# One-hots of a token inversion: GpSimd builds one of the two for six batches of eight, DVE builds the other with wide comparisons

## The chip, the cores and the metric

The kernel runs on one core of one Trainium2 chip. The metric is the device time of one execution in microseconds. Five engines work side by side, each through its own instructions in its own order: TensorE (PE; its weight loads are shown apart as PEld), VectorE (DVE), ScalarE (ACT), GpSimd (POOL) and SyncE (SP, which here only starts DMAs). An instruction waits for what it needs from the others, and everything behind it on its engine waits with it.

## The reference

Eight batches of 3584 tokens with 192 channels go through a causal depthwise convolution, with 7 taps and one softmaxed filter for each of 8 heads. All 28672 convolved tokens then go to a mixture of experts: a token whose skip score is positive goes to the one of 8 experts with the largest logit and has that expert's result, times the gate, added.

```python
def _attn_ref(x, weight):                      # x (8, 3584, 192), weight (8, 7)
...
    out = np.einsum('hk,bskhg->bshg', w, x_unf)
    return out.reshape(B, S, D).astype(np.float32)

def _moe_ref(x, w_skip, w_gate, w1, w2):       # w1 (8, 192, 1024), w2 (8, 1024, 192)
    skip_score = x @ w_skip
    do_compute = skip_score > 0
    out = x.copy()
    xc = x[do_compute]
    logits = xc @ w_gate
    e_idx = np.argmax(logits, axis=1)
...
    for e in range(E):
        mask = e_idx == e
        h = np.maximum(xc[mask] @ w1[e], 0.0)
        y[mask] = gate_w[mask, None] * (h @ w2[e])
    out[do_compute] = xc + y
```

## The kernel before, in words

**Phase 1** has eight steps, one for each batch. A batch lies in SBUF as 30 columns (`NC`) of 120 tokens (`R`), token within the column on the partition. In its step each of the 8 heads is convolved on PE (`pc`, L333, two matmuls a head with a band matrix) and copied by ACT into `ys` (L335); SP loads the input of the batch two steps on (`load_x`, which has two small memsets on POOL, L113 and L114, before its loads L115 to L121) and stores `ys` to the output (`store_y`, L383 and L386). Between the heads of one step stands the work on the batch before: `router` (transposes `tp`, L419; the odd channel parts are first copied to `yc`, by POOL at L398 for batches 0 to 5; logits `pl`, `pb`) and `route` (on DVE: the largest logit, the gate, and by a running count the slot that each token gets in its expert's list). A slot is a row `r` of 128 and a column `q`: `ri`, `qi`, then `rf`, `qf` as floats (L557, L559).

**The inversion** (`invert`) turns "slot of a token" into "token of a slot". For each of the 30 columns of a batch it builds two tables by comparison: `oa` (120 tokens x 128 rows; 1 where the row is the token's row) and `ob` (120 x 144; 1 where the column is the token's). One of the two carries the token's number as value, taken from `vtab` (the program's `vtab32`). The matmul `inv += oa^T ob` (L581) puts each number at its slot in PSUM; 30 matmuls for a batch, accumulating over batches 0 to 4 and then over 5 to 7. Before, DVE builds both: one `tensor_scalar` for each column and table, in groups of four columns (`IC`).

**The order is written by hand.** `invert` and the other pieces are generators; a `yield HOP` ends a turn. The tables `RR`, `IR` and `BGS` say how many turns of routing, of inversion and of background work follow each head, and `PICK` in which order two routings and an inversion take turns. Background work is the preparation of expert weights: load, maximum on DVE (`am`, `ar`), an all-reduce over partitions on POOL (`sc`, L262), powers of two on DVE (L305 to L310), scaled halves on ACT and DVE. In phase 1 it is done for two experts (the all-reduces beside batch 0's inversion and late in step 5). The products of a group of columns come one turn (`lag`) after its tables, in the tail two.

**The tail.** After the inversion of batch 4 (`REL`), lists for two experts (`sidxa`) are cut out, and POOL begins with indirect DMAs: gathers of 128 tokens each (`y`, L739) and of their gates (`g`, L747), after the memsets of their tiles (L726, L727), and later scatters of the results (`out_dram`, L816). Eight blocks of these experts (up-projection `ph` L792 with ACT `hh` and DVE `hl`, down-projection `po` L827 to L842) run on PE while batches 6 and 7 are routed and batches 5 to 7 inverted. Then come the final lists (`sidx`) and **the steady part**, one block behind the other on PE.

## Time and profile before

| | |
|---|---|
| median of 3 runs | 726.39 us (724.96 to 727.82) |
| the profiled execution | 726.94 us, span 724.9 us |
| PE busy, whole span | 675.7 us (93%) |
| DVE busy | 596.3 us (82%) |
| POOL busy | 391.4 us (54%) |
| DVE, tables `oa` and `ob` (240 instructions each) | 59.2 us and 48.7 us |
| PE, matmuls `inv` (240) | 29.9 us |
| start of the memset at the end of step 2 (input of batch 4), and of the first at the end of step 6 (tiles of the tail) | 75.53 us, 184.67 us |

A row of the timeline has the start, the duration, engine, line, operation, output tile<-input tiles, shape and count; in brackets stands the engine's idle time before it and who ended that. A row of the groups has the count, then busy time of all, the mean of one (which overlaps its neighbours, since an engine starts an instruction before the last has ended), and the idle time before them. In a row of the stretches stand the busy times of PE, PEld, DVE, ACT and POOL with their instructions, the clock granted to PE (1.00 is full), the DMA share, and GB/s.

### The profile page before, as it was taken

To read this page: it belongs to the slowest core of one execution; us is meant where nothing else is said; L and a number is where in the kernel's file an instruction comes from. 1 tells how busy PE (TensorE), PEld (TensorE's weight loads), DVE (VectorE), ACT (ScalarE), POOL (GpSimd) and SP (SyncE) were. 2 spreads that over 40 slices of the span, in tenths; PEclk is the share of its full clock that TensorE was granted. 3 is DMA by queue.
4 is the path that set the end of the run, shared out by engine and by line. 5 is a ranking of instruction groups with operands and counts; after the bars stand their busy time and mean duration, and the time that the engine had idled before them with its cause. 6 is when DMAs were issued, how large, how long until landed. Compare 5 with 4: busy or idle time off the path is not lost.

```text
span 724.9 us, 16759 instructions
## 1 busy us (share of the span) xinstructions
PE 675.7 (93%) x5768; PEld 537.6 (74%) x5768; DVE 596.3 (82%) x1917; ACT 319.8 (44%) x654; POOL 391.4 (54%) x434
## 2 busy tenths in 40 slices
PE   5989699798989888999999999999999999999994
PEld 4656466575668778988888888888888888888883
...
GB/s 227 170 268 291 233 241 292 250 211 241 90 213 194 53 110 109 155 112 146 168 123 183 123 165 162 92 174 179 86 180 147 126 127 152 291 279 300 294 181 12
...
## 3 DMA queue, kind: packets, MB, share of 16 engines
...
## 4 chain that ended last, share of the span: by engine, by line
PE 61%; DVE 7%; DMA 1%; ACT 0%; issue 0%; POOL 0%; POOLq 0%; DVEq 0%
PE ph L792 32%; PE po L827 18%; PE po L830 9%; DVE oa L590 2%; PE po L842 2%; DVE ob L596 1%; DVE hl L797 1%; DMA m<-yt 1%; DMA y<-out_dram,sidx 1%; DVE o L813 0%; DVE yt L766 0%; DVE yam L756 0%; PE tp L419 0%; ACT hh L795 0%; PE inv L581 0%
## 5 line engine op out<-in xcount | busy, mean ns | idle before, releaser
L795 ACT ACTIVATE hh<-ph 128x512 f16<-128x512 f32 x230 | 132.9, 590 | 223.7 <-PE ph L792 215.3
L792 PE MATMUL ph<-m,wt 128*128 128x256 f16 (+1 forms) x2000 | 221.0, 269 | 6.0 <-DVE hl L797 4.7
L792 PEld LDWEIGHTS <-wt 128*128 128x128 f16 x2000 | 189.0, 98 | 30.2 <-issue 7.4
L827 PE MATMUL po<-wt,hh 128*128 128x384 f16 x656 | 167.5, 326 | 0.0
L797 DVE SCALAR_TENSOR_TENSOR hl<-ph,hh 128x512 f16<-128x512 f32 x230 | 155.5, 686 | 10.5 <-ACT hh L795 8.9
L830 PE MATMUL po<-wt,hl 128*128 128x192 f16 x656 | 147.5, 246 | 0.0
L827 PEld LDWEIGHTS <-hh 128*128 128x128 f16 x808 | 78.3, 98 | 39.7
L747 POOL DMA_INDIRECT g<-gate_dr,sidx x82 | 87.3, 1065 | 25.0 <-issue 24.1
L739 POOL DMA_INDIRECT y<-out_dram,sidx x82 | 84.1, 1026 | 27.0 <-issue 18.6
L816 POOL DMA_INDIRECT out_dram<-o,sidx x82 | 84.6, 1031 | 25.1 <-issue 5.8
L830 PEld LDWEIGHTS <-hl 128*128 128x128 f16 x808 | 79.1, 98 | 10.2
L333 PE MATMUL pc<-xs,toep 128*120 128x360 f32 x224 | 84.0, 499 | 0.0
L813 DVE SCALAR_TENSOR_TENSOR o<-po,yf,y 128x192 f32<-128x192 f32 x115 | 47.3, 415 | 42.2 <-PE po L827 35.0
L761 ACT ACTIVATE yt<-y,ysc 128x192 f16<-128x192 f32 x115 | 46.4, 447 | 70.5 <-DVE ysc L310 51.8
L335 ACT COPY ys<-pc 120x720 f32<-120x720 f32 x56 | 42.5, 759 | 58.8 <-PE pc L333 37.4
L766 DVE SCALAR_TENSOR_TENSOR yt<-y,ysc,yt 128x64 f16<-128x64 f32 x230 | 58.2, 313 | 1.9 <-ACT yt L761 1.7
L590 DVE TENSOR_SCALAR oa<-iota_r,rf,vtab 120x128 f16<-120x128 f16 x240 | 59.2, 315 | 0.0
L333 PEld LDWEIGHTS pc<-xs,toep 128*120 128x120 f32 x224 | 39.1, 195 | 16.8 <-issue 3.6
L596 DVE TENSOR_SCALAR ob<-iota_q,qf 120x144 f16<-120x144 f16 x240 | 48.7, 264 | 0.0
L813 DVE SCALAR_TENSOR_TENSOR o<-po,yf,o 128x192 f32<-128x192 f32 x101 | 42.2, 418 | 3.6
L286 DVE SCALAR_TENSOR_TENSOR wt<-raw,ar,wt 128x512 f16<-128x512 f32 x56 | 41.6, 744 | 4.1 <-ACT wt L275 4.1
L256 DVE TENSOR_REDUCE am<-raw 128x1 f32<-128x512 f32 x56 | 37.8, 677 | 7.7 <-DMA raw<-in_moe_w_dram 7.4
...
## 6 DMA issues: line engine op xcount, KB each, us to landing
...
```

Source lines behind the costliest of these rows:

```text
L333: nc.tensor.matmul(pc[0:R, i, 0:n * G], toep[:, h, :], xs[:, c0 + n * i:c0 + n * i + n, h * G:(h + 1) * G], start=True, stop=True)
L590: nc.vector.tensor_scalar(out=oa[:, v, :], in0=iota_r[0:R], scalar1=rf[:, c0 + v:c0 + v + 1], scalar2=vtab32[0:R, c0 + v:c0 + v + 1], op0= ...
L739: rows_apart(nc.gpsimd.indirect_dma_start(out=k.y[:, u, :], out_offset=None, in_=out[0:k.rows, :], in_offset=bass.IndirectOffsetOnAxis(ap= ...
L747: nc.gpsimd.indirect_dma_start(out=k.g[:, u:u + 1], out_offset=None, in_=gate_dr[0:k.rows, :], in_offset=bass.IndirectOffsetOnAxis(ap=k.si ...
L766: nc.vector.scalar_tensor_tensor(out=yt[:, u, o:o + b_ - a], in0=k.y[:, u, a:b_], scalar=sc[:, u:u + 1], in1=yt[:, u, a:b_], op0=ALU.mult, ...
L792: nc.tensor.matmul(ph[:, f - f0, :], wt[:, o + f * P:o + (f + 1) * P], k.m[:, m, 0:w], start=(n == 0), stop=(n == len(seq) - 1))
L795: nc.scalar.activation(hh, ph, AF.Relu)
L797: nc.vector.scalar_tensor_tensor(out=k.hl[:, f0:f0 + fs, 0:w], in0=ph, scalar=0.0, in1=hh, op0=ALU.max, op1=ALU.subtract)
L813: nc.vector.scalar_tensor_tensor(out=o[:, u, :], in0=part, scalar=f2[:, u:u + 1], in1=base, op0=ALU.mult, op1=ALU.add)
L816: rows_apart(nc.gpsimd.indirect_dma_start(out=out[0:k.rows, :], out_offset=bass.IndirectOffsetOnAxis(ap=k.si[:, u:u + 1], axis=0), in_=o[: ...
L827: nc.tensor.matmul(po, k.hh[:, f, u * P:(u + 1) * P], w2[:, f], start=(f == 0), stop=(f == NF - 1))
L830: nc.tensor.matmul(po[:, 1], k.hl[:, f, u * P:(u + 1) * P], w2[:, f, 0], start=False, stop=False)
```

## The change

`IC` goes from 4 to 8 columns, worked in two half-turns of four columns, and the tables have three buffers of eight columns instead of four of four. For batches 0 to 5 POOL builds `ob`, one `tensor_scalar` a column, now with the value, so 30 a batch and 180 in all (new L600); DVE builds `oa` with one wide `tensor_tensor` for eight columns (120 x 1024, L609) and no value. For batches 6 and 7 DVE builds both wide: `oa`, `oa` times the value, `ob`. `rf` becomes f16, and so does `qf` in batches 6 and 7; an f16 table of the values is added. The products of a group of eight come after both of its half-turns, four in each turn.

```diff
--- before.py
+++ after.py
@@ -28,7 +28,7 @@
 LAST = S - R * (NC - 1)
 NG = NC // 2
 HALVES = ((0, 16), (16, NC - 16))
-IC = 4
+IC = 8
 SPAN = 32768
 QC = 18
 NQ = E * QC
@@ -63,6 +63,7 @@
 PICK = "102"
 E1 = 3
 PSEQ = (0, 0, 3, 4, 4, 4, 4, 4)
+ONE_HOTS_BY_GPSIMD = (0, 1, 2, 3, 4, 5)
 TLAG = 2
 HOP = -1
 
@@ -204,6 +205,9 @@
                             fill=0.0, base=0, channel_multiplier=1)
     iota_r = const.tile([P, P], F16, name="iota_r")
     iota_q = const.tile([P, NQ], F16, name="iota_q")
+    vtab = const.tile([P, NC], F16, name="vtab")
+    nc.gpsimd.iota(vtab, pattern=[[R, NC]], base=-(S // 2), channel_multiplier=1,
+                   allow_small_or_imprecise_dtypes=True)
     vtab32 = const.tile([P, NC], F32, name="vtab32")
     nc.gpsimd.iota(vtab32, pattern=[[R, NC]], base=-(S // 2), channel_multiplier=1,
                    allow_small_or_imprecise_dtypes=True)
@@ -553,9 +557,9 @@
         nc.vector.tensor_scalar(out=qi, in0=si, scalar1=7, scalar2=None, op0=ALU.arith_shift_right)
         nc.vector.tensor_tensor(out=eq3(cmp), in0=stab, in1=bstart[:, b].unsqueeze(2).broadcast_to([P, E, QC]),
                                 op=ALU.is_ge)
-        rf = t2("rf", F32, 2)
+        rf = t2("rf", F16, 2)
         nc.vector.tensor_copy(rf, ri)
-        qf = t2("qf", F32, 2)
+        qf = t2("qf", F32 if b in ONE_HOTS_BY_GPSIMD else F16, 2)
         nc.vector.tensor_copy(qf, qi)
         rq[b] = (rf, qf, gt)
         if b < B - 1:
@@ -570,37 +574,58 @@
 
     def invert(b, rf, qf, gt):
 
+        def each(table, n):
+            return table[0:R].unsqueeze(1).broadcast_to([R, ic, n])
+
+        def along(t, n):
+            return t[0:R, c0:c0 + ic].unsqueeze(2).broadcast_to([R, ic, n])
+
         lag = TLAG if in_tail else 1
+        by_gpsimd = b in ONE_HOTS_BY_GPSIMD
         due = []
 
         def products(at):
             if due and due[0][0] <= at:
-                _, c0, oa, ob = due.pop(0)
-                for v in range(min(IC, NC - c0)):
+                _, c0, v0, oa, ob = due.pop(0)
+                for v in range(v0, min(v0 + IC // 2, NC - c0)):
                     w = c0 + v
                     nc.tensor.matmul(inv, oa[:, v, :], ob[:, v, :],
                                      start=(b in (0, REL + 1) and w == 0), stop=(b in (REL, B - 1) and w == NC - 1))
 
+        def columns(v0):
+
+            if by_gpsimd:
+                for v in range(v0, min(v0 + IC // 2, ic)):
+                    w = c0 + v
+                    nc.gpsimd.tensor_scalar(out=ob[:, v, :], in0=iota_q[0:R], scalar1=qf[:, w:w + 1],
+                                            scalar2=vtab32[0:R, w:w + 1], op0=ALU.is_equal, op1=ALU.mult)
+
         at = 0
         for c0 in range(0, NC, IC):
             ic = min(IC, NC - c0)
-            oa = wk1.tile([R, IC, P], F16, tag="oa", bufs=4, name=f"oa{b}_{c0}")
-            ob = wk1.tile([R, IC, NQ], F16, tag="ob", bufs=4, name=f"ob{b}_{c0}")
-            for v in range(ic):
-                nc.vector.tensor_scalar(out=oa[:, v, :], in0=iota_r[0:R], scalar1=rf[:, c0 + v:c0 + v + 1],
-                                        scalar2=vtab32[0:R, c0 + v:c0 + v + 1], op0=ALU.is_equal, op1=ALU.mult)
+            oa = wk1.tile([R, IC, P], F16, tag="oa", bufs=3, name=f"oa{b}_{c0}")
+            ob = wk1.tile([R, IC, NQ], F16, tag="ob", bufs=3, name=f"ob{b}_{c0}")
+            columns(0)
+            nc.vector.tensor_tensor(out=oa[:, 0:ic, :], in0=each(iota_r, P), in1=along(rf, P), op=ALU.is_equal)
             if c0 == 0:
                 store_gates(b, gt)
             yield
-            for v in range(ic):
-                nc.vector.tensor_scalar(out=ob[:, v, :], in0=iota_q[0:R], scalar1=qf[:, c0 + v:c0 + v + 1],
-                                        scalar2=None, op0=ALU.is_equal)
+            if not by_gpsimd:
+                nc.vector.tensor_tensor(out=oa[:, 0:ic, :], in0=oa[:, 0:ic, :], in1=along(vtab, P), op=ALU.mult)
             products(at)
-            due.append((at + lag, c0, oa, ob))
+            at += 1
+            yield HOP
+            columns(IC // 2)
+            if not by_gpsimd:
+                nc.vector.tensor_tensor(out=ob[:, 0:ic, :], in0=each(iota_q, NQ), in1=along(qf, NQ), op=ALU.is_equal)
+            products(at)
+            due.extend((at + lag, c0, v0, oa, ob) for v0 in (0, IC // 2))
             at += 1
             yield HOP
         while due:
             products(at)
+            if lag == 1:
+                products(at)
             at += 1
             if due:
                 yield HOP
```

Line numbers with the change are one to four higher up to `invert` (L113 is L114, L262 is L266, L333 is L337, L398 is L402, L419 is L423) and 25 higher behind it (L739 is L764, L816 is L841); L581 is L592.

POOL around the first all-reduce (`sc`), in step 2, before. `ISA` alone is the instruction that loads code for POOL; the one with `sc` is the all-reduce.

```order
50 L398 COPY yc_0_566<-ys_346 120x1024
51 L398 COPY yc_1_595<-ys_346 120x896
52 L262 ISA
53 L262 ISA sc_734<-ar_732 128x2
54 L113 MEMSET xs_810 8x192
55 L114 MEMSET xs_810 32x192
56 L398 COPY yc_0_885<-ys_514 120x1024
```

The same place with the change; the tables `ob` are batch 0's, and the number behind `ob_` is the group's first column.

```order
52 L402 COPY yc_1_597<-ys_348 120x896
53 L600 TENSOR_SCALAR ob_0_638<-iota_q,qf_634,vtab_193 120x144 x8
54 L600 TENSOR_SCALAR ob_8_707<-iota_q,qf_634,vtab_193 120x144 x4
55 L266 ISA
56 L266 ISA sc_720<-ar_718 128x2
57 L600 ISA
58 L600 TENSOR_SCALAR ob_8_707<-iota_q,qf_634,vtab_193 120x144 x4
59 L600 TENSOR_SCALAR ob_16_761<-iota_q,qf_634,vtab_193 120x144 x8
60 L114 MEMSET xs_781 8x192
61 L115 MEMSET xs_781 32x192
62 L600 TENSOR_SCALAR ob_24_824<-iota_q,qf_634,vtab_193 120x144 x4
63 L402 COPY yc_0_853<-ys_516 120x1024
```

The all-reduce and two loads of code now stand in the midst of batch 0's tables, and the memset of the next input behind 24 of its 30 columns. Between the tables of batches 2 and 3 the second all-reduce has such a load on either side too:

```order
82 L600 TENSOR_SCALAR ob_24_1416<-iota_q,qf_1233,vtab_193 120x144 x2
83 L266 ISA
84 L266 ISA sc_1462<-ar_1460 128x2
85 L402 COPY yc_1_1481<-ys_1092 120x896
86 L600 ISA
87 L600 TENSOR_SCALAR ob_0_1527<-iota_q,qf_1523,vtab_193 120x144 x8
```

Before, no load of code stood there, and none before the first all-reduce of the steady part, where one stands now.

POOL at the start of the tail, with the change, from the last gathers of the first row of gathers on; the tables are batch 5's:

```order
119 L764 DMA y_2003<-out_dram,sidxa 128x192
120 L772 DMA g_2000<-gate_dr,sidxa 128x1 x2
121 L764 DMA y_2007<-out_dram,sidxa 128x192 x2
122 L600 TENSOR_SCALAR ob_0_2189<-iota_q,qf_2185,vtab_193 120x144 x8
123 L600 TENSOR_SCALAR ob_8_2281<-iota_q,qf_2185,vtab_193 120x144 x8
124 L600 TENSOR_SCALAR ob_16_2350<-iota_q,qf_2185,vtab_193 120x144 x8
125 L600 TENSOR_SCALAR ob_24_2457<-iota_q,qf_2185,vtab_193 120x144 x6
126 L764 DMA y_2011<-out_dram,sidxa 128x192 x2
127 L841 DMA out_dram<-o_2724,sidxa 17920x192 x2
```

Fifteen gathers stand ahead of batch 5's tables, and the others behind all 30 columns. PE at the place of batch 5's first products in step 7 (`pc_6` is head 6 of batch 7, `pl_1`, `pb` and `tp` batch 6's routing), before:

```order
622 L419 MATMUL tp_1_3_2411<-ident,ys_1806 128x120 x2
...
624 L581 MATMUL inv<-ob_0_2357,oa_0_2356 128x144
...
631 L333 MATMUL pc_5_0_2440<-xs_1798,toep 120x360 x2
632 L450 MATMUL pb_0_2444<-ident,lt_0_2403 120x128 x2
633 L419 MATMUL tp_1_4_2450<-ident,yc_1_2311 128x120 x4
```

And with the change:

```order
622 L423 MATMUL tp_1_3_2240<-ident,ys_1675 128x120 x2
623 L337 MATMUL pc_5_0_2259<-xs_1667,toep 120x360 x2
624 L454 MATMUL pb_0_2263<-ident,lt_0_2232 120x128 x2
625 L423 MATMUL tp_1_4_2269<-ident,yc_1_2143 128x120 x4
626 L423 MATMUL tp_1_5_2275<-ident,yc_1_2143 128x120 x3
...
628 L592 MATMUL inv<-ob_0_2189,oa_0_2188 128x144
...
635 L337 MATMUL pc_6_0_2300<-xs_1667,toep 120x360 x2
```

The first products come one head later than before.

## The prediction

> **What bounds the kernel now.** I read the page's busy shares first, then the stretches of ten microseconds, PE's waits, and last the rows of POOL, because the change moves work onto it.
>
> ```profile
> PE 675.7 (93%) x5768; PEld 537.6 (74%) x5768; DVE 596.3 (82%) x1917; ACT 319.8 (44%) x654; POOL 391.4 (54%) x434
> 80.00:90.00 10.00, 4.80 (x19) 3.80 (x20) 5.88 (x24) 4.78 (x9) 0.00 (x0) 0.67 0.86 249
> 160.00:170.00 10.00, 7.82 (x52) 5.67 (x49) 9.70 (x36) 8.73 (x18) 1.23 (x1) 1.00 1.08 336
> 240.00:250.00 10.00, 7.90 (x68) 6.79 (x68) 9.93 (x42) 1.77 (x4) 3.52 (x4) 0.83 0.15 41
> 260.00:270.00 10.00, 7.59 (x71) 6.23 (x70) 9.83 (x42) 2.36 (x5) 4.09 (x4) 1.00 0.49 116
> 300.00:310.00 10.00, 10.00 (x92) 8.62 (x91) 9.72 (x34) 3.81 (x7) 7.67 (x8) 1.00 0.38 95
> ```
>
> After its length a stretch gives the busy us of PE, PEld, DVE, ACT and POOL, then PE's granted clock and the DMA share. PE is the bound over the whole span, and from about 290 us it runs without gaps (the row at 300 stands for those behind it). Before that it idles: in steps 2 to 6 (48 to 185 us), where the DMA share is near 1 and DVE is often near 10 of 10, and in the tail, where DVE is full until 270 us. So the change can win only before 290 us, by making DVE shorter, and it can lose wherever PE comes to wait for POOL. POOL looks idle in the steps (0.00 and 1.23 of 10), but its work stands at fixed places. PE's waits from 60 to 290 us by releaser, and the rows of the largest:
>
> ```profile
> PE inv L581 <- DVE ob L596: 8.4, 10, 3.4
> PE tp L419 <- ACT ya L420: 6.3, 2, 5.5
> 85.20 1.86 PE L419 MATMUL tp<-ident,ys 120*128 120x120 f32 x8 [5.45 <-ACT ya L420]
> 138.61 0.36 PE L514 MATMUL pr<-oh,ones 120*128 120x240 f16 x1 [1.89 <-DVE oa L590]
> 171.21 0.72 PE L581 MATMUL inv<-ob,oa 120*128 120x144 f16 x4 [3.39 <-DVE ob L596]
> 171.77 2.31 PE L333 MATMUL pc<-xs,toep 128*120 128x360 f32 x4
> ```
>
> The one-hots cost PE 8.4 us of waiting before 290 us. The last row shows what follows a stall: the four matmuls of one head took 2.31 us, against 1.42 us in the rows quoted below.
>
> **The change, part by part.** DVE's part first. The groups of the one-hots, and two wide comparisons of DVE's with f32 operands as the nearest rows for the new form:
>
> ```profile
> L590 DVE TENSOR_SCALAR oa<-iota_r,rf,vtab 120x128 f16<-120x128 f16 x240 | 59.2, 315 | 0.0
> L596 DVE TENSOR_SCALAR ob<-iota_q,qf 120x144 f16<-120x144 f16 x240 | 48.7, 264 | 0.0
> L493 DVE TENSOR_TENSOR df<-lg,lm 120x240 f32<-120x240 f32 x8 | 3.2, 403 | 0.0
> L554 DVE TENSOR_TENSOR cmp<-stab,bstart 128x144 f32<-128x144 f32 x8 | 2.4, 304 | 0.0
> ```
>
> Busy time per instruction is 59.2/240 = 0.247 us and 48.7/240 = 0.203 us, so eight columns cost DVE 8 x 0.450 = 3.60 us now. From the two wide rows an element costs (403 - 304)/96 = 1.03 ns over a fixed 156 ns, so 1024 elements take 1.21 us; were f16 passed at two per cycle, about half, 0.6 us. In batches 0 to 5 DVE thus saves 2.4 us per eight columns, 9.0 us per batch of 30. In batches 6 and 7 it does two passes over 1024 elements and one over 1152 (1.34 us): 3.76 us instead of 3.60, no gain; at two per cycle it would save 1.7. I take the slower end, since nothing here shows a wide f16 operation that repeats an operand.
>
> POOL gets 30 instructions of 144 elements for each of six batches. No such instruction is in the trace; the nearest rows:
>
> ```profile
> L398 POOL COPY yc<-ys 120x1024 f32<-120x1024 f32 x6 | 6.3, 1045 | 1.6 <-ACT ys L335 1.3 <-ACT ys L350 0.3
> L315 POOL COPY hist<-eoff 128x8 f32<-128x8 f32 x1 | 0.2, 212 | 0.0
> L189 POOL TENSOR_TENSOR mk<-mk 128x120 f32<-128x120 f32 x4 | 1.8, 469 | 0.2
> L187 POOL TENSOR_TENSOR mk<-mk 128x360 f32<-128x360 f32 x2 | 1.9, 964 | 0.1
> 144.73 0.91 DVE L557 CAST rf<-ri 120x30 f32<-120x30 int32 x1
> 145.55 0.17 DVE L559 CAST qf<-qi 120x30 f32<-120x30 int32 x1
> ```
>
> By the copies, one pass costs (1045 - 212)/1016 = 0.82 ns per element: 144 elements take about 0.32 us. By the tensor_tensor rows, (964 - 469)/240 = 2.06 ns per element: 0.52 us. Two operations per element put it nearer to the latter: I take 0.5 us a column, 15 us a batch, and keep 0.35 to 0.65 (0.52 stretched by a quarter, as the two engines hold each other up: the cast of 30 elements at 144.73 took 0.91 us, while POOL made a copy, and its like 0.17 us just behind it). From the end of step 2 to that of step 6 (75.5 and 184.67 in rows below) a step lasts 109.2/4 = 27.3 us, so 15 us fit; what counts is when they are ready.
>
> **Reloads.** The change puts two more rows of the kind that stands once before POOL's first all_reduce on either side of it, and does so twice (batch 0 and batch 2), since the comparison and the all_reduce need different code. What such a row costs:
>
> ```profile
> 63.20 0.95 POOL L398 COPY yc<-ys 120x896 f32<-120x896 f32 x1 [13.03 <-PE tp L419]
> L262 POOLq MODIFY_POOL_CONFIG  x2: 5/5/5, 64.4 to 64.4; - x2
> 71.87 0.37 POOL L262 PARTITION_ALL_REDUCE sc<-ar  x1 [7.71 <-DVE ar L260]
> L143 POOLq MODIFY_POOL_CONFIG  x2: 11/11/11, 0.9 to 0.9; - x2
> L143 POOL IOTA rt<- x1: 229/229/229, 9.2 to 9.2; 128x120 f32 x1
> ```
>
> From 0.9 to 9.2 us nothing else held POOL: 8.3 us at most. From 64.4 to the all_reduce at 71.87: 7.5 us at most, and there `ar` was also awaited. I take 7 us, with 0 (fully hidden) and 8.3 as bounds. The Trainium skill's "GPSIMD Engine Reference", section "Instruction dispatch", gives about 6 us for the first call after such a load, with no instruction to show for it; the trace agrees in kind, and at 6 us the sums of the two places below would each be about 2 us smaller.
>
> *Place one, step 2.* Slots of batch 0 are known at 64.3. POOL makes 12 columns (6 us, and 2 us for DVE in its way) until 72.3, reloads until 79.3, reduces, reloads until 86.7, and makes four more columns until 88.7. PE's eight products stand here:
>
> ```profile
> 75.50 0.66 PE L581 MATMUL inv<-ob,oa 120*128 120x144 f16 x8
> 82.59 5.78 SPq L121 DMA_DIRECT2D xs<-in_x_dram  x1
> 88.90 9.45 SPq L386 DMA_DIRECT2D out_dram<-ys  x1
> ```
>
> PE waits from 75.5 to 88.7. It has 4.2 us of work from there to the transposes that now start at 85.20, after a stall of 5.45 us that the new one swallows: 88.7 + 4.2 is 92.9, so **+8 us** (+5 if the reloads take 5 us). The memset of the next input tile stands behind 8 further columns on POOL, at 92.7 instead of about 75.5; the load at 82.59 waits for it, and the store at 88.90 stands behind that load on SP: some 10 us later, in a stretch with the DMAs full. I add **1 us** for it; it could be 5.
>
> *DVE's own waits* in steps 4 and 5 (1.89 us in the row at 138.61, and some small ones) go: **-2 us**, between -3 and 0: batches 1 and 2 meet no reload, and POOL makes their 30 columns within the step.
>
> *Place two, steps 5 and 6.* The second pair of reloads ends with batch 3's first columns. POOL's copy ends at 145.6, the reload at 152.6, four columns at 154.6 and then four every 2 us. The products stand in PE's row at
>
> ```profile
> 152.62 0.41 PE L581 MATMUL inv<-ob,oa 120*128 120x144 f16 x4
> 152.87 1.42 PE L333 MATMUL pc<-xs,toep 128*120 128x360 f32 x4
> 157.28 0.66 PE L581 MATMUL inv<-ob,oa 120*128 120x144 f16 x8
> ```
>
> The first waits 2.0 us, the third 1.3 us more; each is followed by a head or two at the slow clock, some 1 us. Against these 5 us stand the 3.39 us at 171.21, which go with DVE's lighter load. **+1.5 us**, from -2 (0.35 us a column, reload hidden) to +7 (0.65).
>
> *Place three, step 7.* Batch 5's one-hots stand behind POOL's first 15 gathers:
>
> ```profile
> 184.67 0.42 POOL L726 MEMSET y<- 128x384 f32 x1 [17.84 <-PE pc L333]
> 187.66 1.92 POOL L739 DMA_INDIRECT y<-out_dram,sidxa  x1 [0.19 <-POOL g L727]
> 207.08 0.99 POOL L739 DMA_INDIRECT y<-out_dram,sidxa  x1 [0.30 <-issue]
> 194.92 0.18 DVE L559 CAST qf<-qi 120x30 f32<-120x30 int32 x1
> 197.35 0.41 PE L581 MATMUL inv<-ob,oa 120*128 120x144 f16 x4
> ```
>
> The 15th gather ends at 208.1, four columns are ready at 210.1; PE's place, one head later than the row at 197.35, is 199.9. PE stalls 10 us, and loses some 3 us at the slow clock. DVE has 9 us less to do from here and is what the tail waits for (9.93 and 9.83 of 10 in its stretches); the stall also takes the place of idle time that PE has in them. Of 13 us I leave **+3 us**, between 0 and +7 (DVE's relief fully felt, or two thirds of it). The gathers behind batch 5's one-hots come 15 us later; they are for later blocks of the tail, whose earlier blocks cover them, and without that cover the term is at its upper end.
>
> *The tail's reload.* One more row of this kind stands before the first all_reduce of the steady part:
>
> ```profile
> 312.28 0.36 POOL L262 PARTITION_ALL_REDUCE sc<-ar  x1 [1.15 <-DVE ar L260]
> 314.20 0.16 DVE L305 TENSOR_SCALAR sc<-sc 128x2 f32<-128x2 f32 x1
> ```
>
> POOL has come free only at 311.1 (312.28 - 1.15), so with a reload of 7 us the all_reduce ends at 318.5, and the step on DVE that needs it comes 4.3 us after 314.20, with all of DVE's queue behind it. POOL is busy 7.67 of 10 there and DVE 9.72 of 10, so neither catches up soon; PE feels what exceeds its buffered work. **+1 us**, 0 to +4.3.
>
> Sum: 8 + 1 - 2 + 1.5 + 3 + 1 = **+12.5 us**. The profiled execution took 726.94 us (span 724.9), 0.55 us over the median, so it comes to 739.4 by the profile's own time and **739 us** by the median.
>
> **The rivals.**
>
> *No change (727 us).* The stall at place one costs nothing where DMAs are the bound anyway (share 0.86 in the stretch at 80), and the tail takes up step 7's. For it: a 5.45 us stall already stands there. Against: 88.7 is later than 85.2, and work still follows it. It needs reloads of 4 us or less.
>
> *Faster (720 us).* DVE's relief of 9 us in each of six batches is felt: of the 8.4 us of waits on ob 6 go. It needs a column at 0.35 us or wide comparisons at two per cycle, and PE's stall in step 7 given back in full. Against: three of the six batches meet a reload or the gathers.
>
> *Slower, POOL sets the pace (765 us).* At 1 us a column a batch takes 30 us on POOL, and 33 with copies and memsets, against 27 us a step: 6 us on each of five steps, 30, and the reloads' 8. Nothing in the rows above is that slow; it decides from 0.8 us on.
>
> *Slower, DVE and POOL shut each other out (751 us).* In a step DVE would be busy 9.7 - 3.3 = 6.4 of 10 (a stretch less 9.0/27) and POOL (15 + 2)/27 = 6.3 of 10. Where all of it excludes one another, 12.7 must fit into 10; if half of DVE's operations do, steps stretch by some 3 us in four of them: 12 us on top. For it: the cast at 144.73. The Trainium skill's "SBUF — State Buffer", section "SBUF: two separate sides", has this as a rule: a DVE operation with two SBUF inputs, against a GpSimd one that reads SBUF, takes the shared ports for its whole length and the other blocks; the wide comparison is such an operation.
>
> **How the numbers follow.** The forecast has 0.46, no change 0.17, faster 0.13, shutting out 0.14, POOL's pace 0.10. The half-widths of its terms (5 for place one with the DMAs, 1.5, 4.5, 3.5 and 2) as independent ones give the root of 64, 8 us: its own range is 731 to 747. The range to hold 8 in 10 goes from 723, which cuts off most of the faster case, to 757, which takes in shutting out. Runs of this kernel tell about 0.5% from no change: 722.8 to 730.0 is "same". Faster 0.13; same 0.17; slower 0.46 + 0.14 + 0.10 = 0.70.
>
> **What would show it.** Place one: POOL's all_reduce near 79.5 instead of 71.9, an idle row of 10 us or more on PE's `inv` near the end of step 2, released by POOL's `ob`, and the next input memset near 92. Place two: two or three such rows of 1 to 2 us, and none of 3.39 us in step 6. Place three: one row of 8 to 11 us, released by POOL's `ob`, behind the 15th gather. DVE's `oa` at 1.1 to 1.2 us for 1024 elements, POOL's `ob` at 0.5 us. The prediction is wrong if PE's idle time before 291 us is less than now, if a reload takes under 4 us, or if the steady part from 320 us on has another pace than now.

## The result: 807 us instead of 727, 11% slower

The kernel with the change took 807.14 us (median of 4 runs, 805.5 to 808.25), the one before in the same rounds 727.11 us: ratio 1.110, 95% interval 1.106 to 1.114. The forecast was 739 us, with a range to 757. The profiled execution took 805.5 us, span 803.8 us.

From the page of the kernel after: busy shares, POOL's slices, the chain of waits that ended last, and the groups of the one-hots.

```profile
PE 694.0 (86%) x5768; PEld 546.2 (68%) x5768; DVE 560.7 (70%) x1485; ACT 321.6 (40%) x654; POOL 566.2 (70%) x615
POOL 5206599957998972567577777777777777777642
PE 57%; POOL 22%; DVE 7%; issue 6%; SPq 3%; DMA 3%; ACT 1%; POOLq 0%; DVEq 0%; ACTq 0%
PE ph L817 28%; POOL ob L600 19%; PE po L852 16%; PE po L855 8%; SPq L390 2%; PE po L867 2%; DMA raw<-in_moe_w_dram 1%; DVE oa L609 1%; PE pp L350 1%; DVE hl L822 1%; PE tp L423 1%; DVE ob L620 1%; POOL yc L402 1%; PE pc L337 1%; DMA xs<-in_x_dram 1%
L600 POOL TENSOR_SCALAR ob<-iota_q,qf,vtab 120x144 f16<-120x144 f16 x180 | 170.2, 959 | 16.4 <-issue 15.4
L592 PE MATMUL inv<-ob,oa 120*128 120x144 f16 x240 | 35.9, 244 | 64.3 <-POOL ob L600 58.5
PE tp L423 <- POOL yc L402: 14.3, 4, 5.1
```

POOL had 0% of the chain before and has 22% now, 19 points of it in the columns of `ob`. They took 170.2 us for 180, 0.96 us on the mean, and PE waited 58.5 us for them. It waited 14.3 us more (four times, 5.1 us at most) for the copies `yc`, which the transposes of the next batch need and which now stand behind columns on POOL; before, it never waited for them. The stretches show where (PE, PEld, DVE, ACT, POOL, then clock, DMA share, GB/s):

```profile
80.00:90.00 10.00, 0.00 (x0) 0.00 (x0) 5.41 (x14) 0.00 (x0) 1.25 (x3) 0.50 0.95 272
150.00:160.00 10.00, 8.62 (x74) 5.83 (x72) 4.31 (x9) 5.78 (x15) 10.00 (x13) 1.00 0.42 119
230.00:240.00 10.00, 6.89 (x42) 3.45 (x41) 0.00 (x0) 1.21 (x4) 10.00 (x13) 0.62 0.00 0
260.00:270.00 10.00, 1.69 (x12) 1.14 (x11) 3.20 (x9) 2.06 (x6) 8.15 (x9) 0.75 0.76 172
```

PE does nothing at all from 80 to 90 us; later POOL is full (10.00) while DVE has nothing to do (0.00 at 230). The bound of phase 1 has gone from PE, DMA and DVE to POOL. The three places of the prediction, POOL's rows first, then PE's:

```profile
62.48 11.61 POOL L600 TENSOR_SCALAR ob<-iota_q,qf,vtab 120x144 f16<-120x144 f16 x12 [0.62 <-DVE qf L563]
80.29 0.37 POOL L266 PARTITION_ALL_REDUCE sc<-ar  x1 [6.21 <-issue]
89.12 9.97 POOL L600 TENSOR_SCALAR ob<-iota_q,qf,vtab 120x144 f16<-120x144 f16 x12 [8.46 <-issue]
177.49 0.37 POOL L266 PARTITION_ALL_REDUCE sc<-ar  x1 [6.02 <-PE pg L570]
185.64 21.78 POOL L600 TENSOR_SCALAR ob<-iota_q,qf,vtab 120x144 f16<-120x144 f16 x24 [6.90 <-issue]
216.97 27.66 POOL L600 TENSOR_SCALAR ob<-iota_q,qf,vtab 120x144 f16<-120x144 f16 x30
267.87 26.57 POOL L600 TENSOR_SCALAR ob<-iota_q,qf,vtab 120x144 f16<-120x144 f16 x30
```

```profile
90.03 0.28 PE L592 MATMUL inv<-ob,oa 120*128 120x144 f16 x1 [15.68 <-POOL ob L600]
90.87 0.28 PE L592 MATMUL inv<-ob,oa 120*128 120x144 f16 x1 [0.56 <-POOL ob L600]
186.55 0.28 PE L592 MATMUL inv<-ob,oa 120*128 120x144 f16 x1 [4.52 <-POOL ob L600]
268.78 0.28 PE L592 MATMUL inv<-ob,oa 120*128 120x144 f16 x1 [7.65 <-POOL ob L600]
```

The reloads stand on either side of the all-reduce as the order has them (6.21 and 8.46 us, then 6.02 and 6.90). PE waits 15.68 us at place one and 7.65 us behind the gathers at place three. After each long wait it takes one product per column, 0.84 us apart (90.03, 90.87): a whole batch of 30 columns took POOL 27.66 us.

To see what each stretch of the program lost I use step lengths: from the first `pc` matmul of a batch to the first of the next batch; step 7 to its last `pc`; the tail from there to the write of `sidx`; then the rest. In us:

```
                     2     3     4     5     6     7    tail   rest
before             27.8  32.0  22.9  26.9  26.9  21.1  65.3  453.8
after              46.5  33.3  30.2  43.3  45.4  32.3  74.7  451.9
```

Steps 2 to 6 have 62.2 us of the loss, step 7 has 11.2, the tail 9.4. The steady part has none, although the third reload stands there.

The 62 us can be read from POOL's own rows. From batch 0's first column (62.48 us) to the end of batch 4's last (216.97 + 27.66 = 244.63) it is 182.2 us, and POOL is never free in them but for gaps of 1.0 us together: 143.5 us are the 150 columns, 27.6 the four loads, and 10.0 the copies, memsets and all-reduces. In the kernel before, the same piece of the program, from batch 0's slots at 64.3 to the first memset of the tail at 184.67, lasts 120.4 us. The difference is 61.8 us: in steps 2 to 6 the kernel lasts as long as POOL's work does.

The kernel before took 855 us on one of the chips that the experiments ran on and 864 us on another, 128 and 137 us more than here, which every kernel traced there loses from the first gathers on, for a reason that is not known; runs from there are read by their steps 2 to 6, whose sum agrees with that on other chips to 3 us. What depends on the total was run again on another chip.

### The profile page after: what moved, and what is told of

Its sections match the earlier page's. It is cut to its first block, busy times and chain, and to the rows that moved or that the text cites. A ratio compares the mean times of both kernels' runs of the same rounds, so it can differ in the third digit from the quotient of the medians.

```text
span 803.8 us, 16513 instructions
## 1 busy us (share of the span) xinstructions
PE 694.0 (86%) x5768; PEld 546.2 (68%) x5768; DVE 560.7 (70%) x1485; ACT 321.6 (40%) x654; POOL 566.2 (70%) x615
## 4 chain that ended last, share of the span: by engine, by line
PE 57%; POOL 22%; DVE 7%; issue 6%; SPq 3%; DMA 3%; ACT 1%; POOLq 0%; DVEq 0%; ACTq 0%
PE ph L817 28%; POOL ob L600 19%; PE po L852 16%; PE po L855 8%; SPq L390 2%; PE po L867 2%; DMA raw<-in_moe_w_dram 1%; DVE oa L609 1%; PE pp L350 1%; DVE hl L822 1%; PE tp L423 1%; DVE ob L620 1%; POOL yc L402 1%; PE pc L337 1%; DMA xs<-in_x_dram 1%
## 5 line engine op out<-in xcount | busy, mean ns | idle before, releaser
L600 POOL TENSOR_SCALAR ob<-iota_q,qf,vtab 120x144 f16<-120x144 f16 x180 | 170.2, 959 | 16.4 <-issue 15.4
L841 POOL DMA_INDIRECT out_dram<-o,sidx x82 | 86.3, 1052 | 25.1 <-issue 4.9
L764 POOL DMA_INDIRECT y<-out_dram,sidx x82 | 82.9, 1011 | 25.4 <-issue 17.1
L337 PE MATMUL pc<-xs,toep 128*120 128x360 f32 x224 | 92.7, 542 | 0.0
L592 PE MATMUL inv<-ob,oa 120*128 120x144 f16 x240 | 35.9, 244 | 64.3 <-POOL ob L600 58.5
L339 ACT COPY ys<-pc 120x720 f32<-120x720 f32 x56 | 42.5, 760 | 116.4 <-PE pc L337 91.4
L786 ACT ACTIVATE yt<-y,ysc 128x192 f16<-128x192 f32 x115 | 46.4, 448 | 75.6 <-DVE ysc L314 64.6
L838 DVE SCALAR_TENSOR_TENSOR o<-po,yf,y 128x192 f32<-128x192 f32 x115 | 47.3, 415 | 39.8 <-PE po L852 32.4
L337 PEld LDWEIGHTS pc<-xs,toep 128*120 128x120 f32 x224 | 42.5, 212 | 30.4 <-issue 17.2
L592 PEld LDWEIGHTS <-oa 120*128 120x128 f16 x240 | 21.6, 106 | 61.2 <-issue 59.4
L290 DVE SCALAR_TENSOR_TENSOR wt<-raw,ar,wt 128x512 f16<-128x512 f32 x56 | 41.8, 746 | 27.8 <-ACT wt L279 27.8
```

Source lines behind the costliest of these rows:

```text
L337: nc.tensor.matmul(pc[0:R, i, 0:n * G], toep[:, h, :], xs[:, c0 + n * i:c0 + n * i + n, h * G:(h + 1) * G], start=True, stop=True)
L592: nc.tensor.matmul(inv, oa[:, v, :], ob[:, v, :], start=(b in (0, REL + 1) and w == 0), stop=(b in (REL, B - 1) and w == NC - 1))
L600: nc.gpsimd.tensor_scalar(out=ob[:, v, :], in0=iota_q[0:R], scalar1=qf[:, w:w + 1], scalar2=vtab32[0:R, w:w + 1], op0=ALU.is_equal, op1=AL ...
L764: rows_apart(nc.gpsimd.indirect_dma_start(out=k.y[:, u, :], out_offset=None, in_=out[0:k.rows, :], in_offset=bass.IndirectOffsetOnAxis(ap= ...
L841: rows_apart(nc.gpsimd.indirect_dma_start(out=out[0:k.rows, :], out_offset=bass.IndirectOffsetOnAxis(ap=k.si[:, u:u + 1], axis=0), in_=o[: ...
```

## The experiments

Theories: **P**, the price of a column on POOL was set too low, and POOL's pace is the loss; **R**, the reloads; **L**, DVE and POOL hold each other up; **G**, batch 5 behind the gathers; **H**, the half-turns and wide forms cost time themselves.

**All tables on DVE, wide.** No batch on POOL; the rest of the change stays.

```diff
-ONE_HOTS_BY_GPSIMD = (0, 1, 2, 3, 4, 5)
+ONE_HOTS_BY_GPSIMD = ()
```

> All eight batches take the form of batches 6 and 7: DVE builds both tables wide, POOL none; half-turns and groups of eight stay. Theory P (POOL's columns, 0.83 to 0.96 us each, set the pace of every step, and the reloads come on top): all of the 80 us is POOL's, and with DVE at 1.245 + 1.225 + 1.35 = 3.82 us per eight columns instead of 3.60 the time is 727, within 5 us of before. Rival H (the half-turns and the later products cost time themselves, because PE's order has changed): 735 or more, with waits on ob or oa in the steps.

On the 855 us chip: ratio 1.002 (0.997 to 1.006). So it was run again:

> No table on POOL, all wide on DVE, the half-turns as in the change. All of the loss was POOL's: ratio 0.995 to 1.01, as on the slower chip (1.0016). If DVE's wide form, 3.82 us instead of 3.60 per eight columns, counts where DVE is full: 1.005 to 1.015, with waits on oa and ob in steps 6 and 7.

734.42 us against 726.65: ratio 1.011 (1.008 to 1.014), the second of the two cases. Nine tenths of the loss go with POOL's part, but not all: 7.8 us stay with nothing on POOL, in steps 5 and 6 (2.5 and 3.6 us) and above all in the tail (73.2 us instead of 65.3), less what other stretches gained. DVE's three passes over eight columns in this run:

```profile
L620 DVE TENSOR_TENSOR ob<-iota_q,qf 120x1152 f16<-120x1152 f16 x24 | 32.4, 1350 | 0.0
L614 DVE TENSOR_TENSOR oa<-oa,vtab 120x1024 f16<-120x1024 f16 x24 | 31.6, 1315 | 0.8
L609 DVE TENSOR_TENSOR oa<-iota_r,rf 120x1024 f16<-120x1024 f16 x24 | 30.2, 1257 | 0.0
PE inv L592 <- DVE ob L620: 20.5, 15, 3.0
```

Together (32.4 + 31.6 + 30.2)/24 = 3.93 us, 0.33 more than before, in pieces of 1.3 us for which everything else on DVE waits; PE waits 20.5 us for them.

**The forms mixed, on DVE.** The wide comparison for `oa`, a `tensor_scalar` a column for `ob`, which brings the value; all eight batches, nothing on POOL.

```diff
-ONE_HOTS_BY_GPSIMD = (0, 1, 2, 3, 4, 5)
+ONE_HOTS_BY_GPSIMD = (0, 1, 2, 3, 4, 5, 6, 7)
...
-                    nc.gpsimd.tensor_scalar(out=ob[:, v, :], in0=iota_q[0:R], scalar1=qf[:, w:w + 1],
+                    nc.vector.tensor_scalar(out=ob[:, v, :], in0=iota_q[0:R], scalar1=qf[:, w:w + 1],
```

> POOL builds nothing; for all eight batches DVE builds oa with the wide comparison and ob with a tensor_scalar a column that brings the value. DVE per eight columns: 1.22 + 8 x 0.22 = 3.0 us instead of 3.60, 2.2 us less a batch. If DVE's load is what makes PE wait (8.4 us before 290 us in the kernel before): ratio 0.993 to 0.998. Rival H (the products come a turn later and in groups of eight, which costs as much): 0.998 to 1.01.

722.45 us against 724.72: ratio 0.997 (0.995 to 0.9997), faster than both kernels, just.

```profile
L600 DVE TENSOR_SCALAR ob<-iota_q,qf,vtab 120x144 f16<-120x144 f16 x240 | 62.7, 338 | 0.0
L609 DVE TENSOR_TENSOR oa<-iota_r,rf 120x1024 f16<-120x1024 f16 x24 | 29.2, 1218 | 0.0
```

That is 29.2/24 + 8 x 62.7/240 = 3.31 us per eight columns, 0.29 less than before. The turns and the order of the products are the same as with all tables wide; only DVE's form differs, and the tail takes 66.0 us instead of 73.2. So with all tables wide the tail's 8 us come with the wide passes in DVE. The half-turns and the cheaper form together cost nothing that can be measured; what the half-turns cost alone is not shown by this run.

The same forms in the old turns of four columns:

```diff
-        rf = t2("rf", F32, 2)
+        rf = t2("rf", F16, 2)
...
-            for v in range(ic):
-                nc.vector.tensor_scalar(out=oa[:, v, :], in0=iota_r[0:R], scalar1=rf[:, c0 + v:c0 + v + 1],
-                                        scalar2=vtab32[0:R, c0 + v:c0 + v + 1], op0=ALU.is_equal, op1=ALU.mult)
+            nc.vector.tensor_tensor(out=oa[:, 0:ic, :], in0=iota_r[0:R].unsqueeze(1).broadcast_to([R, ic, P]),
+                                    in1=rf[0:R, c0:c0 + ic].unsqueeze(2).broadcast_to([R, ic, P]), op=ALU.is_equal)
...
-                                        scalar2=None, op0=ALU.is_equal)
+                                        scalar2=vtab32[0:R, c0 + v:c0 + v + 1], op0=ALU.is_equal, op1=ALU.mult)
```

> The kernel before in its own turns of four columns, but DVE builds oa for four columns with one wide comparison (512 elements, 0.7 us instead of 0.99) and brings the value with ob's tensor_scalar. DVE saves 1.5 us a batch or more. If groups of eight and half-turns neither cost nor bring anything, the time is that of the version with eight columns: ratio 0.995 to 0.999. If the later products of the eight cost something: 0.990 to 0.995.

Ratio 1.003 (0.999 to 1.007) on the 864 us chip, which is neither of the two cases: both had it faster. Its steps 2 to 6 (28.2, 31.6, 22.8, 28.0, 26.9) are those of before within 1.1 us each. So what the half-turns cost by themselves stays open.

**Half the columns.** POOL gets the amount of work that the prediction had assumed.

```diff
-                    nc.gpsimd.tensor_scalar(out=ob[:, v, :], in0=iota_q[0:R], scalar1=qf[:, w:w + 1],
+                    (nc.gpsimd if v - v0 < IC // 4 else nc.vector).tensor_scalar(out=ob[:, v, :], in0=iota_q[0:R], scalar1=qf[:, w:w + 1],
```

> Of every four columns POOL builds two and DVE the other two, one tensor_scalar each with the value. POOL's work per batch is then 16 columns at 0.83 to 0.96 us, 13 to 15 us, which is what the prediction took for all 30. Theory P (only the price of a column was wrong in the prediction): the time is the forecast's 739, between 731 and 747. Rival L (the order, the reloads and DVE and POOL shutting each other out cost more than the sum gave): 755 or more.

862.16 us on the 855 us chip, ratio 1.012 (1.006 to 1.017); steps 2 to 6 are 38.7, 23.5, 22.6, 31.4 and 29.2 us, 8.9 more than before together. Again, for its total:

> Of every four columns POOL builds two, DVE the other two: 16 columns a batch on POOL, 15 to 17 us with what holds them up, which is the work that the prediction assumed. Steps 2 to 6 together were 8.9 us longer than before. Theory P (only the price of a column was wrong): the forecast, 731 to 747, ratio 1.01 to 1.03. Rival (step 7 and the tail add what the other chip hid): 750 or more.

750.33 us against 726.65: ratio 1.032 (1.030 to 1.034), 23.7 us more. Of the 80 us, 56 go with half of POOL's columns: P is the main cause. But the forecast's own +12.5 is not reached either; by the text above it is the rival that came true, if barely (750 or more). By steps against before: 11.4, -9.2, -0.3, 2.4, 1.9 (6.2 together), step 7 +9.9, tail +2.8. Its two long waits:

```profile
88.37 0.28 PE L592 MATMUL inv<-ob,oa 120*128 120x144 f16 x1 [10.61 <-POOL ob L600]
217.43 0.28 PE L592 MATMUL inv<-ob,oa 120*128 120x144 f16 x1 [9.49 <-POOL ob L600]
```

The first, in step 2, is nearly paid back in step 3, which is 9.2 us shorter than before, where the stall of 5.45 us on the stores of `ys`, which the kernel before has there, is gone. The second, behind the gathers, is not paid back.

**What a column costs.** In batches 0 to 5 DVE builds `oa` by columns with the value (`rf` is f32 there again), and POOL's `ob` has one operation.

```diff
-                                            scalar2=vtab32[0:R, w:w + 1], op0=ALU.is_equal, op1=ALU.mult)
+                                            scalar2=None, op0=ALU.is_equal)
...
-            nc.vector.tensor_tensor(out=oa[:, 0:ic, :], in0=each(iota_r, P), in1=along(rf, P), op=ALU.is_equal)
+            if by_gpsimd:
+                for v in range(ic):
+                    nc.vector.tensor_scalar(out=oa[:, v, :], in0=iota_r[0:R], scalar1=rf[:, c0 + v:c0 + v + 1],
+                                            scalar2=vtab32[0:R, c0 + v:c0 + v + 1], op0=ALU.is_equal, op1=ALU.mult)
...
```

> DVE builds oa as before the change, a tensor_scalar a column with the value; POOL builds ob with one operation a column (the comparison alone). Theory L: a wide comparison with two operands in SBUF holds POOL's column up for its whole length, a tensor_scalar does not; so POOL's columns, 0.96 us on the mean, come at their undisturbed price, and the mean lies within 0.05 us of the shortest. Theory P1 (the price of a column goes by its operations): 0.4 to 0.5 us with one operation, and the time 730 to 750 by the first chip's measure (ratio 1.00 to 1.03). Rival P0 (the price goes by the instruction and its elements): 0.8 us again, and with 21 us less of holding up the ratio falls from 1.11 to 1.08 to 1.10 only.

759.3 us against 724.72: ratio 1.047 (1.043 to 1.051). The columns, shortest, median and longest, first in the kernel after, then here:

```profile
L600 POOL TENSOR_SCALAR ob<-iota_q,qf,vtab x180: 833/844/2182, 62.5 to 293.4; 120x144 f16<-120x144 f16 x180
```

```profile
L600 POOL TENSOR_SCALAR ob<-iota_q,qf x180: 630/641/1791, 63.3 to 245.6; 120x144 f16<-120x144 f16 x180
L600 POOL TENSOR_SCALAR ob<-iota_q,qf 120x144 f16<-120x144 f16 x180 | 119.9, 684 | 17.0 <-issue 7.1 <-DMA xs<-in_x_dram 7.0 <-DVE qf L563 2.5
```

One operation less saves 203 ns (844 - 641); two thirds of the price stay. Neither P1 (0.4 to 0.5 us) nor P0 (0.8 again) had that. The mean, 684 ns, lies 54 above the shortest, close to the 50 that L allows; in the kernel after it lies 126 above.

How much of a column goes by its elements this run does not show, but POOL has one other `tensor_scalar`, with one operation on 8 elements (f32, with a constant as scalar). First its row in the kernel before, then in the kernel after:

```profile
L220 POOL TENSOR_SCALAR eoff<-eoff 128x8 f32<-128x8 f32 x1 | 0.4, 353 | 0.1
L224 POOL TENSOR_SCALAR eoff<-eoff 128x8 f32<-128x8 f32 x1 | 0.3, 294 | 0.1
```

So some 0.3 us are there with hardly any elements, and an estimate from 294 and 641 ns gives 2.6 ns for each further element, if type and kind of scalar make no difference, which was not tried.

**Only DVE's form undone.** In batches 0 to 5 `oa` by `tensor_scalar` (the comparison alone, `rf` in f32); POOL's `ob` keeps both operations.

```diff
-            nc.vector.tensor_tensor(out=oa[:, 0:ic, :], in0=each(iota_r, P), in1=along(rf, P), op=ALU.is_equal)
+            if by_gpsimd:
+                for v in range(ic):
+                    nc.vector.tensor_scalar(out=oa[:, v, :], in0=iota_r[0:R], scalar1=rf[:, c0 + v:c0 + v + 1],
+                                            scalar2=None, op0=ALU.is_equal)
...
```

> The kernel after, in which only DVE's form of oa is undone for batches 0 to 5: a tensor_scalar a column (the comparison alone) instead of the wide comparison; POOL keeps its two operations a column. Theory L: POOL's column goes from 0.96 to 0.86 us on the mean (0.827 undisturbed), 18 us over 180 columns, and as POOL is the chain in steps 2 to 7 the time falls by about as much: 785 to 792, ratio 1.08 to 1.09, although DVE has more to do. Rival (the longer columns are the price of the f16 form itself, or lie in waits): 800 or more, mean above 0.93 us.

On the 864 us chip the ratio was 1.064 (1.056 to 1.072); steps 2 to 6 were 11.7 us shorter than in after. Again:

> The kernel after with oa by a tensor_scalar a column. Steps 2 to 6 were 11.7 us shorter so, the tail 3. If that reaches the end: 790 to 797, ratio 1.088 to 1.098. If not: 800 or more.

794.43 us against 724.21: ratio 1.098 (1.095 to 1.102). That is 12.7 us less than after, or 9.8 if each is taken against the kernel before on its own chip (70.2 us more here, 80.0 there); with the groups

```profile
L600 POOL TENSOR_SCALAR ob<-iota_q,qf,vtab 120x144 f16<-120x144 f16 x180 | 160.3, 905 | 15.8 <-issue 14.5 <-DVE qf L563 0.8
L611 DVE TENSOR_SCALAR oa<-iota_r,rf 120x128 f16<-120x128 f16 x180 | 38.0, 297 | 0.0
```

POOL's mean went from 959 to 905 ns and the kernel became faster, though the same table costs DVE more by columns: 38.0 us for batches 0 to 5, against 0.75 x (29.9 + 8.5) = 28.8 us of the wide form (six of eight batches of the two groups of `oa`, 1024 and 768 elements wide). L holds, though the mean fell less than it expected. In the kernel after one sees it row by row, POOL's rows first:

```profile
104.44 2.69 POOL L600 TENSOR_SCALAR ob<-iota_q,qf,vtab 120x144 f16<-120x144 f16 x2
169.80 1.67 POOL L600 TENSOR_SCALAR ob<-iota_q,qf,vtab 120x144 f16<-120x144 f16 x2
105.20 1.21 DVE L609 TENSOR_TENSOR oa<-iota_r,rf 120x1024 f16<-120x1024 f16 x1
L609 DVE TENSOR_TENSOR oa<-iota_r,rf 120x1024 f16<-120x1024 f16 x24 | 29.9, 1245 | 0.0
```

Two columns took 1.67 us where DVE was doing something else, and 2.69 us where a wide comparison of 1.21 us ran beside them. A least-squares fit of the 180 columns against what DVE did meanwhile gives, over a base of 0.83 us, 0.86 us more for each microsecond of a wide comparison, 0.45 for `wt` (also two operands in SBUF), 0.06 for the other `tensor_tensor` (two f32 or mixed operands in SBUF), and, in the runs that have them, -0.2 to +0.15 for the `tensor_scalar` of the tables. The Trainium skill, "SBUF — State Buffer", section "SBUF: two separate sides", has the rule: a DVE operation with two SBUF inputs and a GpSimd operation that reads SBUF shut each other out for a whole instruction. The trace agrees for the wide comparison (0.86); for `wt` it holds only half, and for the other `tensor_tensor` hardly at all (0.06 here, 0.25 in the run above).

**Without the loads.**

```diff
-        nc.gpsimd.partition_all_reduce(sc, ar, P, bass.bass_isa.ReduceOp.max)
+        if e < NA:
+            nc.gpsimd.tensor_copy(sc, ar)
+        else:
+            nc.gpsimd.partition_all_reduce(sc, ar, P, bass.bass_isa.ReduceOp.max)
```

> The kernel after, but for the first two experts POOL copies each partition's own maximum instead of reducing over partitions, which leaves the reduction out (their scales, and so their results, are wrong) and needs no loading of code. Theory P+R: POOL is the one chain in steps 2 to 6, so the four loads (6.2, 8.5, 6.0 and 6.9 us, 27.6 together) come out of the time nearly whole: 775 to 783, with the steps from batch 2's and batch 5's first conv 12 to 15 us shorter each and the others as they are. Rival: POOL's columns alone fill the steps, and the loads lie mostly in waits that are there anyway: 795 or more.

On the 855 us chip (ratio 1.044, 1.034 to 1.054) steps 2 and 5 were 32.8 and 30.9 us, 13.7 and 12.4 shorter than in after, the others as they were to 0.8 us. Again:

> The kernel after, in which for the first two experts each partition's own maximum is copied instead of reduced over partitions (the reduction is left out; their scales are wrong). Steps 2 and 5 were 13.7 and 12.4 us shorter so. If that reaches the end: 778 to 784, ratio 1.07 to 1.08. If DVE, which has its whole work of the tail left, takes it back: 790 or more.

781.41 us against 724.21: ratio 1.079 (1.076 to 1.081), 25.7 us less than after, or 22.8 against each chip's own kernel before; steps 2 and 5 had 33.2 and 31.3 us. R holds: the four loads (27.6 us in the rows above) lie on the chain nearly whole.

**Batch 5 on DVE.**

```diff
-ONE_HOTS_BY_GPSIMD = (0, 1, 2, 3, 4, 5)
+ONE_HOTS_BY_GPSIMD = (0, 1, 2, 3, 4)
```

> Batch 5's tables are built by DVE, so nothing of POOL stands behind the first 15 gathers but gathers. Theory G (place three of the prediction): step 7 and the tail up to the final lists lose what they had gained, 11 and 9 us: 787 to 792. Rival: step 7 and the tail are long because of what DVE has to do after the delays before, and DVE now has 4 us more per eight columns: 800 or more.

On the 855 us chip it took 912 and 928 us, too far apart to compare. Again:

> The kernel after with batch 5's tables built by DVE. Theory G (batch 5's columns behind 15 gathers make step 7 and the tail longer): steps 1 to 6 as in after, step 7 at 21 to 25 us instead of 32.3 and the tail at 66 to 72 instead of 74.7: 787 to 795, ratio 1.083 to 1.095. Rival (the tail is longer because PE comes to it with DVE's work left over): step 7 shorter, the tail longer by as much, 803 or more.

794.77 us against 724.21: ratio 1.098 (1.096 to 1.101), 12.4 us less than after (9.5 against each chip's own kernel before), just outside G's interval of ratios. Step 7 is back at 20.7 us (21.1 before), but the tail takes 73.1, hardly less than the 74.7 of after. So for step 7 G holds: the place behind the gathers costs it 11 to 12 us. For the tail it does not, and the stretches of the tail show why (before, mixed forms, all wide on DVE, batch 5 on DVE, after):

```profile
205.80:271.10 65.30, 57.68 (x578) 49.72 (x577) 63.70 (x266) 24.76 (x56) 18.27 (x18) 0.95 0.50 143
203.40:269.40 66.00, 55.25 (x589) 48.88 (x588) 64.08 (x204) 25.02 (x57) 22.66 (x20) 0.97 0.56 147
210.20:283.40 73.20, 59.11 (x595) 51.39 (x594) 70.96 (x149) 25.12 (x57) 25.90 (x21) 0.93 0.47 133
266.97:340.00 73.03, 55.94 (x594) 48.84 (x593) 70.82 (x148) 24.82 (x57) 25.76 (x21) 0.98 0.51 134
277.10:351.80 74.70, 58.89 (x595) 50.38 (x594) 66.32 (x140) 24.68 (x56) 41.10 (x37) 0.95 0.42 117
```

In the first four DVE is busy in all but 1.6 to 2.2 us: the tail is as long as DVE's work in it, and that is 7 us more where batch 5 is wide on DVE as well. In the kernel after it is 2.6 us more than before, but DVE is idle for 8.4 us there; in that tail PE waits 5.2 us for batch 5's columns, and DVE 6.8 us for `hh` of ACT, which comes from PE's products. So the tail is long in both runs, for different reasons.

**All three together.** `oa` by columns and no loads first, and then batch 5 on DVE too:

> The run before with, for the first two experts, a copy of each partition's own maximum on POOL in place of the reduction over partitions (left out; their scales are wrong), which needs no loading of code. The loads took 6.2, 8.5, 6.0 and 6.9 us there. Theory R (they lie on the chain nearly whole): 25 to 30 us less than the run before, 757 to 765, ratio 1.04 to 1.055, with steps 2 and 5 each 11 to 14 us shorter. Rival (POOL's columns fill what the loads leave): less than 15 us.

> The run before with batch 5's tables built by DVE, so that no column stands behind gathers. Theory G: 7 us less in step 7 and some 5 more in the tail: 745 to 753, ratio 1.025 to 1.037. Rival (the tail makes up for step 7 anyway): within 3 us of the run before. What is left over the kernel before is then the price of the columns of batches 0 to 4 alone.

Both ran on the 864 us chip (ratios 1.036, 1.028 to 1.044, and 1.027, 1.019 to 1.035). Steps 2 and 5 went from 43.5 and 42.5 us to 30.9 and 28.7 with the loads gone; batch 5 changes steps 2 to 6 by 0.4 us together. The second again:

> The kernel after with oa by column, without the loads (the reduction over partitions is left out for the first two experts; their scales are wrong) and with batch 5's tables on DVE. If the three add up (12.7, 25.7 and 12.4 us from 807): 756, between 752 and 760, ratio 1.038 to 1.05; the 25 to 33 us left over the kernel before are the columns of batches 0 to 4 at 0.83 us, which end later than PE's places in every step. If they overlap (POOL's time saved is used only once): 762 or more.

760.33 us against 726.65: ratio 1.047 (1.044 to 1.049). The three save 46.8 us together; one by one it was 12.7 + 25.7 + 12.4 = 50.8. Against each chip's own kernel before it is 46.4 us together and 9.8 + 22.8 + 9.5 = 42.1 one by one. So they add up, as far as times from different chips can tell. Left are 33.7 us: 25.0 in steps 2 to 6 and 7.9 in the tail, where DVE is busy for 70.9 of 73.1 us. For the 25 us POOL's rows for batch 0's first 12 columns and for batch 4:

```profile
65.26 10.22 POOL L603 TENSOR_SCALAR ob<-iota_q,qf,vtab 120x144 f16<-120x144 f16 x12 [0.84 <-DVE qf L566]
184.76 25.79 POOL L603 TENSOR_SCALAR ob<-iota_q,qf,vtab 120x144 f16<-120x144 f16 x30
```

From 65.26 to 184.76 + 25.79 = 210.55 it is 145.3 us, 133.5 of them columns and 1.9 idle, so 24.9 us more than the 120.4 of the kernel before. The 25.0 us are thus the length of POOL's own work; 15 of them fall in step 6, in which batch 4's columns have to be done. The same count, POOL's stretch less 120.4 us, agrees with what steps 2 to 6 lose in the other runs with 30 columns a batch: 61.8 and 62.2 us in after, 51.4 and 51.3 with `oa` by columns, 35.4 and 36.6 without the loads, 20.8 and 20.8 with one operation.

**Where POOL was to have nothing in the way.** The mixed forms, with two of every four columns of `ob` on POOL in batches 1, 2 and 4 alone:

```diff
-ONE_HOTS_BY_GPSIMD = (0, 1, 2, 3, 4, 5)
+ONE_HOTS_BY_GPSIMD = (1, 2, 4)
...
-        by_gpsimd = b in ONE_HOTS_BY_GPSIMD
+        by_gpsimd = True
+        half = IC // 4 if b in ONE_HOTS_BY_GPSIMD else 0
...
-                    nc.gpsimd.tensor_scalar(out=ob[:, v, :], in0=iota_q[0:R], scalar1=qf[:, w:w + 1],
+                    (nc.gpsimd if v - v0 < half else nc.vector).tensor_scalar(out=ob[:, v, :], in0=iota_q[0:R], scalar1=qf[:, w:w + 1],
```

> As the run before, but in batches 1, 2 and 4, whose columns stand between no loads of code and ahead of no gathers, POOL builds two of every four columns of ob. POOL has 16 columns a batch, 14 us. If the loads' and gathers' places were what was left of the loss with half the columns (1.2% there): ratio 0.99 to 1.00, not slower than the run before. Rival L (POOL's columns are still held up by the wide comparison, and PE waits on them): 1.005 or more, with waits on POOL's ob in steps 3, 4 and 6.

733.36 us against 724.72: ratio 1.012 (1.008 to 1.015), 11 us slower than with nothing on POOL. That is the rival's time, but not by what the rival names: steps 3 and 6 are longer than before (37.8 and 31.6 us), as the code has to be loaded for the comparison there as well, between the copies and the first column (7.8 and 7.0 us until that), and PE waits.

```profile
102.88 0.28 PE L593 MATMUL inv<-ob,oa 120*128 120x144 f16 x1 [3.51 <-POOL ob L601]
104.94 0.52 PE L593 MATMUL inv<-ob,oa 120*128 120x144 f16 x3 [1.78 <-POOL ob L601]
L601 POOL TENSOR_SCALAR ob<-iota_q,qf,vtab 120x144 f16<-120x144 f16 x48 | 47.4, 997 | 16.3 <-DVE oa L610 7.8 <-issue 7.0 <-DVE qf L563 1.3
```

**The kernel before, once more,** for its steps on another chip:

> The kernel before once more, for its trace on this chip: on the chip of the last runs it took 855 us where it had taken 727 on the first one. Every theory: the same order and the same step lengths (17.8, 27.8, 32.0, 22.9, 26.9 and 26.9 us from one batch's first conv to the next); if the chip is a slow one again, the difference lies in the stretches in which GpSimd issues gathers and scatters, not in steps 1 to 5.

725.36 us, steps 2 to 7 at 27.8, 32.0, 23.0, 26.6, 27.0 and 21.0 us, tail 65.3: the measure is good to some tenths. This chip was neither of the two, so where those lose their time is read from the other kernels alone.

## Why the prediction was wrong

The direction was right, and so were the places that were named: PE waiting at the end of step 2, in steps 5 and 6, and behind the gathers, and the reloads where the order put them. The mechanism was not: the sum treats these places as separate stalls of a POOL that has time to spare between them, while POOL is hardly ever free from batch 0 to batch 4. So steps 3, 4 and 6, which have no load, lose 27.1 us too. The size was wrong by six times, for these reasons in order.

*The price of a column.* The step that failed is "two operations per element put it nearer to the latter: I take 0.5 us a column", with 0.35 to 0.65 for bounds. It measured 0.83 us undisturbed and 0.96 on the mean. The rows used were of other forms, a copy and a `tensor_tensor`, and "no such instruction is in the trace" overlooked the one `tensor_scalar` that POOL has there: 0.35 us for 8 elements with one operation (L220, shown above). With the slope of the `tensor_tensor` rows, 2.06 ns, 136 elements more make an estimate of 0.63 us, which is what one operation measured; that the second adds 0.20 us no row of the kernel before showed. With half the columns 56 of the 80 us are gone. The consequence was in the text, as the rival in which POOL sets the pace: it was said to decide from 0.8 us on, to be unlikely, and to give 765. It did decide. Its 30 us for the steps fit: POOL's stretch without the loads is 34 us longer than the 120.4 us it has to fit into. Its time was short since it had 8 us for the reloads, which took 27.6, and nothing for the gathers and the tail.

*The reloads.* Each was taken at 7 us; they took 6.2, 8.5, 6.0 and 6.9. The Trainium skill's "GPSIMD Engine Reference", section "Instruction dispatch", says about 6 us for such a load; the two ahead of the all-reduces agree (6.2 and 6.0), the two back to the comparison are up to 2.5 us longer (8.5 and 6.9). The sum had "+8 us" and "1 us" for place one, with all that stands there, and "+1.5 us" for place two; without the loads alone, step 2 is 13.3 us shorter than in after and step 5 12.0. That sum let POOL catch up behind the reloads, which needs time to spare that 0.5 us a column leaves and 0.9 does not. In the run with half the columns steps 2 and 3 together lose 2.2 us and steps 5 and 6 4.3.

*Place three.* "Of 13 us I leave +3" failed: 9.5 to 12.4 us are got back when batch 5 is not on POOL, and with half the columns step 7 alone lost 9.9. The stall itself was close (10 us said, 7.65 in one row). I had let the tail pay 10 us back because DVE would have 9 us less to do from here. It has not: from step 7 to `sidx` it was busy for 81.8 us before and 82.2 after.

*The tail.* The sum had nothing for it but what place three and the reload in the steady part leave; it lost 9.4 us. *The wide passes of batches 6 and 7,* "no gain" and nothing in the sum, are a part of that at most: DVE's work in the tail is 2.6 us more than before, and the rest is DVE idle, behind PE and batch 5's columns. Only with batch 5 wide on DVE too is it 7 us more. No run undid the passes of batches 6 and 7 alone. Their duration was right (1.21 us expected for 1024 elements, 1.245 measured).

*DVE and POOL shutting each other out* was a rival at 12 us; it measures 10 to 13, on top of the rest, not in place of it. That the figure fits is luck: the rival had half of DVE's operations hold POOL up in four steps, and the fit shows it for the wide comparison nearly in full, for `wt` in half and for hardly anything else.

*The copies `yc`* were in no term. They stand behind columns on POOL, and PE waited 14.3 us for them, on the same chain, so this is not to be added to the rest.

*DVE's own waits,* -2 us: they went, but PE waited for POOL in the same steps, and steps 4 and 5 are 7.3 and 16.4 us longer. The steady part's reload, +1 us: nothing (451.9 us from `sidx` on, 453.8 before).

Ledger of the 80 us: reloads 23 to 26, batch 5 behind the gathers 10 to 12, wide comparisons beside POOL's columns 10 to 13 (the lower ends against each chip's own kernel before; together 46 to 47 measured), and 33.7 left: 25 in steps 2 to 6, POOL's pace with columns at 0.9 us, and 8 in the tail, DVE's work with the wide passes of three batches.
